# Reordering the first loads of a fused SSM and SwiGLU kernel

## The chip, the cores and the metric

The kernel runs on one core of one Trainium2 chip. The metric is the device time of one execution in microseconds (us); less is better. Three runs of the kernel before gave 200.62, 200.81 and 201.20 us, a median of 200.81 us.

## What is computed

A block of 2048 tokens with 512 features is normalized, and the normalized rows go through two branches whose results are added to the input:

```python
xn = layernorm(x)                                   # x: 2048 x 512, bf16
Lam_bar = exp(dt * Lam)                             # branch A: a diagonal complex state space model
Bu = xn @ B_bar.T                                   # 512 states
h[t] = Lam_bar * h[t-1] + Bu[t]                     # scan over the 2048 tokens
y = 2 * real(h @ C.T) + xn * Dskip
gate, up = xn @ w1, xn @ w3                         # branch B: 512 -> 1792, twice
glu = (silu(gate) * up) @ w2                        # 1792 -> 512
out = x + y + glu
```

All of it depends on the layer normalization, and the first thing that TensorE can do with data needs a piece of x, its statistics, and a piece of w1.

## The kernel before

The tokens are cut into four blocks of 512 (`TBLK`), each of four chunks of 128 tokens (`CPB`); the 1792 columns of w1 and w3 are cut into 14 tiles of 128 (`NFT`). For each block the GLU (`glu`, L587) multiplies the transposed, normalized block `xnT` by each tile of w1 and of w3 (four matmuls of 512 columns each), ScalarE takes the two sums out of PSUM (L596 with Silu, L597), VectorE multiplies them (L604). Between tiles stand the matmuls of the state space branch (`bu`), and behind block pairs the output products (`y_fast`). The order on each engine is written by hand in program order (`manual_schedule`); background work of VectorE is put between by a planner (`Filler`) with fixed costs. No order depends on when a transfer lands.

Block 0 is special, since nothing is there yet when it starts. Its first three tiles (`FIRST = 3`) are computed in quarters, chunk by chunk, as the data comes (`quarter`, L619). The order on the engines is this:

- VectorE: statistics of chunk 0 (L219, L220), of chunk 1, then the normalization (`ln_apply`, L224) of chunk 0 in two halves and of chunk 1, then statistics of chunks 2 and 3, then the normalization of chunks 2 and 3.
- ScalarE: its own DMA issues, a table load (L199), then Ln and Exp for 1/sqrt(variance) of each chunk (L233, L234), copies of the transposed chunks from PSUM to `xnT` (L244). After the first Exp comes an activation (L173) that writes one element of w1's later columns; the next weight load on SyncE's queue must wait for it, and so does all that SyncE issues behind it (`bulk_loads`).
- TensorE: ten matmuls on constants (`keep_busy`, L196), the transposes of chunk 0 (L243), four small ones on constants, the transposes of chunk 1, then L619 for chunk 0 on tiles 0 and 1 (eight matmuls with w1, eight with w3), for chunk 1 on the same tiles (16), the transpose of the state space parameters (L315), the transposes of chunk 2, chunk 0 on tile 2 (four with w1, four with w3), the transposes of chunk 3, chunk 1 on tile 2, and then chunks 2 and 3 on all three tiles. From tile 3 on the full width is used (L587).
- GpSimd: constants, three small loads of the state space parameters, and the parameters' arithmetic.

Loads are issued by two engines, SyncE (SP) and ScalarE (ACT); each issue takes its engine's queue some 0.4 to 0.5 us, and the data comes behind it on the 16 DMA engines. `load_w(f0, f1)` loads the columns f0 to f1 of w1 (L156) and of w3 (L157), by default both on SyncE's queue; with `0, 2 * P` that is tiles 0 and 1, with `2 * P, 4 * P` tiles 2 and 3, each piece 256 KB in runs of 512 bytes. A chunk of x is 128 KB in rows of 1 KB; chunks 0 and 1 are loaded in column halves. The first loads before are, in each queue's order:

| queue | loads |
|---|---|
| SyncE | chunk 0 left half, chunk 1 left half (L166), chunk 2 (L168), w1 then w3 of tiles 0 and 1, w1 then w3 of tiles 2 and 3 |
| ScalarE | chunk 0 right half, chunk 1 right half (L166), chunk 3 (L167) |

Behind these come, on SyncE's queue, w1 and w3 of tiles 4 to 7, block 1 of x (L162), the state space matrices by transposing DMA (L176, L177), the rest of w1 and w3, and so on. The loads share eight semaphores in turn, so each load from the ninth on waits, before it is issued, for the landing of the one eight places before it.

Of the kernel before, what the change touches and what calls it, by code (L numbers as in the profile page):

```python
# [17 lines left out]
P = 128  # L18
# [45 lines left out]
def kernel(  # L64
# [17 lines left out]
    nc = tc.nc  # L82
    _, S, D = A_x.shape
# [21 lines left out]
    D1, D2 = slice(0, DH), slice(DH, D)  # L105
# [3 lines left out]
    xv = A_x[0].rearrange("(c p) d -> p c d", p=P)  # L109
# [41 lines left out]
    x_blk = [x_all[:, i] for i in range(NBLK)]  # L151
# [3 lines left out]
    def load_w(f0, f1, eng1=nc.sync, eng3=nc.sync):  # L155
        eng1.dma_start(out=w1_sb[:, :, f0:f1], in_=w1v[:, :, f0:f1])  # L156
        eng3.dma_start(out=w3_sb[:, :, f0:f1], in_=w3v[:, :, f0:f1])  # L157
# [3 lines left out]
        for i in range(0, CPB, n):  # L161
            nc.sync.dma_start(out=x_blk[b][:, i:i + n, :], in_=xv[:, b * CPB + i:b * CPB + i + n, :])  # L162

    for c in range(2):
        for eng, dsl in ((nc.sync, slice(0, D // 2)), (nc.scalar, slice(D // 2, D))):
            eng.dma_start(out=x_blk[0][:, c, dsl], in_=xv[:, c, dsl])  # L166
    nc.scalar.dma_start(out=x_blk[0][:, 3, :], in_=xv[:, 3, :])  # L167
    nc.sync.dma_start(out=x_blk[0][:, 2, :], in_=xv[:, 2, :])  # L168
    load_w(0, 2 * P)
    load_w(2 * P, 4 * P)  # L170

    def bulk_loads():
# [1110 lines left out]
```

## Time and profile before

| what | value |
|---|---|
| median of three runs | 200.81 us (200.62 to 201.20) |
| profiled execution: span from the first to the last instruction | 199.5 us |
| median of the runs less that span | 1.3 us |
| granted clock of TensorE | 0.999 |
| busy share of the span: TensorE / VectorE / ScalarE / GpSimd | 98% / 91% / 68% / 26% |
| data moved by DMA | 25.12 MB, mean 126 GB/s |
| first matmul on data (L243) / first L619 / first L587 | 5.08 / 6.27 / 12.88 us |

The profile is of one execution; its page names its span and not a time of the whole execution, so the 1.3 us around the span are taken from the runs. PE in the views is TensorE, PEld its weight load, DVE is VectorE, ACT ScalarE, POOL GpSimd, SP SyncE; a q behind an engine's name is its queue. A timeline line gives the start, the time to the end, the engine, the line of the kernel, the operation, what it writes and reads, how many were merged, and in brackets how long the engine was idle before and what ended it. "DMA to landing" counts from the start of the issue to the last of the data.

### The profile page before, as it was taken

To read this page: it belongs to the slowest core of one execution; us is meant where nothing else is said; L and a number is where in the kernel's file an instruction comes from. 1 tells how busy PE (TensorE), PEld (TensorE's weight loads), DVE (VectorE), ACT (ScalarE), POOL (GpSimd) and SP (SyncE) were. 2 spreads that over 40 slices of the span, in tenths; PEclk is the share of its full clock that TensorE was granted. 3 is DMA by queue.
4 is the path that set the end of the run, shared out by engine and by line. 5 is a ranking of instruction groups with operands and counts; after the bars stand their busy time and mean duration, and the time that the engine had idled before them with its cause. 6 is when DMAs were issued, how large, how long until landed. Compare 5 with 4: busy or idle time off the path is not lost.

```text
span 199.5 us, 3700 instructions
## 1 busy us (share of the span) xinstructions
PE 195.6 (98%) x1401; PEld 130.7 (65%) x1401; DVE 181.8 (91%) x254; ACT 135.0 (68%) x281; POOL 51.5 (26%) x75
## 2 busy tenths in 40 slices
PE   8999999999999999999999999999999999999994
PEld 2774444444444488866555468888566678888893
DVE  3689699999999999989999997999999999999972
ACT  4699897699999996968998684362588783111220
POOL 7180289700411134041202305040021303310000
PEclk9999999999999999999999999999999999999999
DMA  4999996991497054730997455838137732941111
GB/s 138 326 277 200 302 186 124 343 273 23 69 181 141 0 105 82 135 105 0 156 148 119 89 92 98 172 83 132 53 59 129 149 56 52 174 92 36 53 44 40
DMA packets 32258, 25.12 MB, mean 126 GB/s; under 512 B 16240, under 2 KB 29936, under 8 KB 32240
## 3 DMA queue, kind: packets, MB, share of 16 engines
q0 software_dynamic: 6128, 11.38, 33.5%
q1 hardware_dynamic: 25536, 13.21, 26.8%
q10 hardware_dynamic: 576, 0.30, 0.5%
q8 instruction: 11, 0.18, 0.4%
q14 instruction: 7, 0.06, 0.1%
HBM read 7.74 MB, written 2.10 MB: 49 GB/s over the span
## 4 chain that ended last, share of the span: by engine, by line
PE 95%; DMA 2%; SPq 1%; issue 0%; DVE 0%
PE gu_ps L587 34%; PE gu_ps L1054 17%; PE y_ps L1054 10%; PE gu_ps L848 7%; PE bu_ps L1054 7%; PE bu_ps L454 3%; PE y_ps L454 3%; PE y_ps L869 3%; PE y_ps L780 3%; DMA w_sb<-in_B_w_dram 2%; PE gu_ps L619 2%; PE gu_ps L780 2%; PE bu_ps L869 1%; PE bu_ps L780 1%; PE bu_ps L619 1%; SPq L166 0%
## 5 line engine op out<-in xcount | busy, mean ns | idle before, releaser
L587 PE MATMUL gu_ps<-xnT,w_sb 128*128 128x512 bf16 x312 | 69.6, 379 | 0.0
L587 PEld LDWEIGHTS <-w_sb 128*128 128x128 bf16 x312 | 30.5, 98 | 34.2
L1054 PEld LDWEIGHTS <-act 128*128 128x128 f16 x462 | 43.5, 98 | 5.4
L596 ACT ACTIVATE g<-gu_ps 128x512 bf16<-128x512 f32 x41 | 24.8, 606 | 6.0 <-PE gu_ps L587 3.6
L597 ACT ACTIVATE u<-gu_ps 128x512 bf16<-128x512 f32 x41 | 24.8, 606 | 4.5 <-PE gu_ps L587 3.7
L505 DVE TENSOR_TENSOR_SCAN u<-rho,ends,u 128x512 bf16<-128x512 f32 x16 | 20.0, 1270 | 0.0
L527 POOL DMA_DIRECT2D act<-p x7 | 9.2, 1320 | 34.0 <-DVE act L519 22.1
L1054 PE MATMUL gu_ps<-w_sb,act 128*128 128x256 bf16 (+3 forms) x126 | 16.0, 267 | 0.0
L848 PE MATMUL gu_ps<-xnT,w_sb 128*128 128x512 bf16 x64 | 15.9, 379 | 0.0
L604 DVE TENSOR_TENSOR act<-g,u 128x1024 f16<-128x1024 bf16 x21 | 14.2, 679 | 0.4 <-ACT u L597 0.4
L860 ACT ACTIVATE g<-gu_ps 128x512 bf16<-128x512 f32 x14 | 8.4, 599 | 5.4 <-PE gu_ps L848 5.0
L454 PEld LDWEIGHTS <-bt 128*128 128x128 bf16 x64 | 6.3, 98 | 7.5
L1077 ACT ACTIVATE x_blk<-gu_ps 128x256 f32<-128x256 f32 (+1 forms) x9 | 3.3, 368 | 10.6 <-PE gu_ps L1054 10.6
L1054 PE MATMUL bu_ps<-w_sb,act 128*128 128x256 bf16 (+3 forms) x84 | 10.4, 264 | 0.0
L1054 PE MATMUL gu_ps<-ct,act 128*128 128x256 f16 (+1 forms) x72 | 10.4, 267 | 0.0
L848 PEld LDWEIGHTS <-w_sb 128*128 128x128 bf16 x64 | 6.3, 98 | 4.8
L505 DVE TENSOR_TENSOR_SCAN u<-rho,u 128x512 bf16<-128x512 f32 x8 | 9.2, 1206 | 0.0
L1054 PEld LDWEIGHTS <-x_blk 128*128 128x128 f16 x88 | 8.6, 98 | 1.0
L1054 PEld LDWEIGHTS <-tw 128*128 128x128 f16 x88 | 8.6, 98 | 1.0
L513 DVE TENSOR_TENSOR p<-u,tabe 128x2048 f16<-128x2048 bf16 (+1 forms) x8 | 8.7, 1085 | 0.1
L519 DVE TENSOR_TENSOR act<-u,tabe 128x2048 f16<-128x2048 bf16 (+1 forms) x8 | 8.7, 1083 | 0.0
L488 DVE TENSOR_TENSOR u<-u,tabe 128x2048 bf16<-128x2048 bf16 x7 | 8.5, 1219 | 0.1
(203 smaller groups left out, 392.5 us busy)
## 6 DMA issues: line engine op xcount, KB each, us to landing
act<-p POOLq DMA_DIRECT2D x6, 512.0 KB, 6.1
xn<-x_blk POOLq DMA_DIRECT2D x4, 512.0 KB, 5.5
out_dram<-xn SPq DMA_DIRECT2D x15, 128.0 KB, 1.7
w_sb<-in_B_w_dram SPq DMA_DIRECT2D x1, 1792.0 KB, 8.2
act<-act POOLq DMA_DIRECT2D x5, 352.0 KB, 4.6
w_sb<-in_B_w_dram SPq DMA_DIRECT2D x2, 768.0 KB, 6.4
u<-p POOLq DMA_DIRECT2D x3, 512.0 KB, 5.1
w_sb<-in_B_w_dram SPq DMA_DIRECT2D x4, 256.0 KB, 4.9
```

The source lines that it names most:

```text
L454: nc.tensor.matmul(out=ps, lhsT=bt[:, ri, dt, pt * P:(pt + 1) * P], rhs=xnT_blk[b][:, dt, :], start=(dt == 0), stop=(dt == NDT - 1))
L505: nc.vector.tensor_tensor_scan(out=v, data0=rho[:, pt:pt + 1].to_broadcast([P, TBLK]), data1=v, initial=init, op0=ALU.mult, op1=ALU.add)
L513: nc.vector.tensor_tensor(out=by_state(st["p16"][:, csl]), in0=by_chunk(st["g"][:, :, ::-1, tsl]), in1=by_chunk(tabe[:, psl, 2:0:-1, tsl]) ...
L519: nc.vector.tensor_tensor(out=by_state(act_state(b, hf)[:, csl]), in0=by_chunk(st["g"][:, :, :, tsl]), in1=by_chunk(tabe[:, psl, 0:1, tsl] ...
L527: gp.dma_start(out=a, in_=p16, accum_op=ALU.add)
L587: nc.tensor.matmul(out=ps[:, tsl], lhsT=w[:, dt, f * P:(f + 1) * P], rhs=xnT[:, dt, tsl], start=(dt == 0), stop=(dt == NDT - 1))
L596: nc.scalar.activation(out=g16[:, f % 2, :], in_=g_ps, func=ACT.Silu)
L597: nc.scalar.activation(out=u16[:, f % 2, :], in_=u_ps, func=ACT.Copy)
L604: nc.vector.tensor_tensor(out=act_gates(b, f - 1), in0=split(g16), in1=split(u16), op=ALU.mult)
L780: nc.tensor.matmul(out=out[:, h * TH:(h + 1) * TH], lhsT=left[:, h, k, :], rhs=right[:, k, :], start=(start and h == 0 and k == 0), stop=( ...
L848: nc.tensor.matmul(out=ps, lhsT=w[:, dt, f * P:(f + 1) * P], rhs=xnT[:, dt, :], start=(dt == 0), stop=(dt == NDT - 1))
L1054: nc.tensor.matmul(out=out, lhsT=left[:, k, :], rhs=right[k][:, cols], start=(start and k == 0), stop=(k == NK - 1), skip_group_check=True)
```

## The change

The first loads get another order and partly another queue. The sizes and the total are unchanged, but chunk 1 comes as one load instead of two halves, so there is one load less. Nothing else is changed: the order of the instructions on TensorE, VectorE and GpSimd and of the computing ones on ScalarE is that of before.

```diff
-    for c in range(2):
-        for eng, dsl in ((nc.sync, slice(0, D // 2)), (nc.scalar, slice(D // 2, D))):
-            eng.dma_start(out=x_blk[0][:, c, dsl], in_=xv[:, c, dsl])
-    nc.scalar.dma_start(out=x_blk[0][:, 3, :], in_=xv[:, 3, :])
-    nc.sync.dma_start(out=x_blk[0][:, 2, :], in_=xv[:, 2, :])
-    load_w(0, 2 * P)
+    def load_chunk(c, eng, dsl=slice(0, D)):
+        eng.dma_start(out=x_blk[0][:, c, dsl], in_=xv[:, c, dsl])
+
+    load_chunk(0, nc.sync, D1)
+    load_chunk(0, nc.scalar, D2)
+    load_chunk(1, nc.scalar)
+    load_w(0, 2 * P, nc.sync, nc.scalar)
+    load_chunk(2, nc.sync)
+    load_chunk(3, nc.sync)
     load_w(2 * P, 4 * P)
```

The queues' new order:

| queue | loads |
|---|---|
| SyncE | chunk 0 left half, w1 of tiles 0 and 1, chunk 2, chunk 3, w1 then w3 of tiles 2 and 3 |
| ScalarE | chunk 0 right half, chunk 1, w3 of tiles 0 and 1 |

Line numbers behind the change are higher by three in the changed kernel (L619 becomes L622, and so on).

## The prediction

> **What bounds the kernel now.** I read first the waits of TensorE over the whole execution, because the chain that ended last is 95% PE:
>
> ```profile
> PE 95%; DMA 2%; SPq 1%; issue 0%; DVE 0%
> ...
> PE bu_ps L196 <- PEq L1267: 0.8, 1, 0.8
> PE gu_ps L619 <- DMA w_sb<-in_B_w_dram: 0.3, 1, 0.3
> PE y_ps L243 <- DVE xn L224: 0.2, 1, 0.2
> ...
> PEld L619 <- DMA w_sb<-in_B_w_dram: 0.6, 2, 0.4
> ```
>
> These are all of its waits but for weight loads behind the warm-up and before the first transposes. None lies after 10 us: from there to 197 us TensorE is never listed as waiting, so a stall removed at the head should reach the end in full, and one added there as well. Only the first 10 us matter. Next, the timeline of TensorE there, on which L619 is the GLU of block 0 on its first three tiles:
>
> ```profile
> 5.86 0.40 PE L243 MATMUL y_ps<-ident,xn 128*128 128x128 bf16 x4
> 6.27 0.62 PE L619 MATMUL gu_ps<-xnT,w_sb 128*128 128x128 bf16 x8
> 7.16 1.51 PE L619 MATMUL gu_ps<-xnT,w_sb 128*128 128x128 bf16 x24 [0.27 <-DMA w_sb<-in_B_w_dram]
> 8.61 0.18 PE L315 MATMUL y_ps<-ident,par_rows 12*128 12x12 bf16 x1
> 8.71 0.40 PE L243 MATMUL y_ps<-ident,xn 128*128 128x128 bf16 x4
> 8.95 0.74 PE L619 MATMUL bu_ps<-xnT,w_sb 128*128 128x128 bf16 x8
> ```
>
> Eight such matmuls take 0.45 us elsewhere (24 in 7.16 to 8.61 are 0.06 each). So there are three weight stalls: 0.18 before 6.27 (transposes through at 6.09), 0.44 before 7.16, and a hidden one in the last line, where the same eight matmuls are 0.74 long instead of 0.61: 0.13. They answer to landings. Issue start plus time to landing gives w1 of tiles 0, 1: 2.11+4.1 = 6.2; w3: 2.58+4.5 = 7.1; w1 of tiles 2, 3: 3.13+5.2 = 8.3; w3: 3.69+5.6 = 9.3. The rows, L156 (w1), L157 (w3), then L168 (chunk 2, issued 1.64) and L167 (chunk 3, 1.65):
>
> ```profile
> DMA to landing us min/median/max: 4.1/5.2/5.9
> ...
> DMA to landing us min/median/max: 4.5/5.6/6.9
> ...
> DMA to landing us min/median/max: 3.7/3.7/3.7
> ...
> DMA to landing us min/median/max: 4.0/4.0/4.0
> ```
>
> The sum to win is 0.18+0.44+0.13 = **0.75 us**, but the third stall is the catch: whatever comes before it, TensorE can't pass 9.3 until the second w3 piece has landed. Last, what the DMA engines did (the last two columns are their busy share and GB/s):
>
> ```profile
> 2.00:3.00 1.00, 1.00 (x4) 0.44 (x3) 0.00 (x0) 0.87 (x1) 1.00 (x3) 1.00 1.15 272
> 3.00:4.00 1.00, 1.00 (x4) 0.29 (x2) 0.89 (x3) 0.41 (x1) 0.93 (x3) 1.00 0.47 154
> 4.00:5.00 1.00, 0.92 (x3) 0.15 (x1) 0.96 (x4) 0.85 (x4) 0.61 (x3) 1.00 0.82 250
> 5.00:6.00 1.00, 0.91 (x11) 0.60 (x12) 0.89 (x4) 0.92 (x4) 0.00 (x0) 1.00 1.13 329
> ```
>
> From 5 us on they are full (about 0.31 MB per us); between 3 and 5 they idled (1-0.47)+(1-0.82) = 0.71 us. The second w3 piece ends a queue of 1.5 MB (x 512 KB, four weight pieces of 256 KB); the change alters the order within it, not its size.
>
> **The change part by part.** *Issues.* SyncE issues six loads up to the second w3 piece instead of seven (about 0.45 us each), so the first w1 piece goes out at 1.17 instead of 2.11, the second pair at about 2.6 and 3.1 instead of 3.13 and 3.69. ScalarE still issues three; the third now is a weight piece, which took 0.51 on SyncE against 0.45 for chunk 3. Its table load starts at 2.2 instead of 2.13 and ends by 3.5; the first Ln waits until 4.09 (0.68 idle), which hides it. There is one DMA less, so each later load waits for another of the first ones (the ninth from the start on waits for the one eight before it). The second w3 piece waits for half of chunk 0 (lands by 3), block 1's x for w1's first piece: 6.2 at the latest, against an issue at 6.05, and its data is read at 18. SyncE waits for ScalarE's activation of 4.65 to 4.85 either way, so everything from 4.88 on keeps its time. No compute instruction is added or moved.
>
> *First weights.* w1 by its old time to landing: 1.17+4.1 = 5.3, below the 6.09 at which TensorE wants it. w3 by its own: 1.65+4.5 = 6.15, below 6.54. Even if neither ran faster than before, the first two stalls go: TensorE reaches the parameter transpose at 7.99 instead of 8.61 (its rows land at 2.78+4.5 = 7.3, in time).
>
> *What is late next.* It would then want the second w3 piece at 9.17-0.62 = 8.55; the old time is 9.3. If the DMA engines idle as long as before, that landing stays and the whole 0.62 is handed back as one wait: gain 0. If they don't idle at all, it comes 0.71 earlier, 8.6: gain 0.7, with the bound of 0.75. For the idle's end: a weight piece stands on each queue by 2 us, while before chunks 2 and 3 stood there with weights behind them. Against it: chunks of 1 KB rows are among what moves then in both orders, and nothing shows what the idle came from. I take half, **0.35 us**, bounds 0 and 0.7.
>
> [...]
>
> *Chunk 1 whole on ScalarE's queue.* Its halves landed 2.1 to 2.4 after issue, by 3.5; VectorE takes it at 3.90, after chunk 0. Bounds for the whole: 2.1 (it lands at 3.3) and that of w3, 4.5 (5.7). Nearest are chunk 0's halves, which have its place in the queue, and chunk 3, which has its shape (4.0, so 5.1). I take 4.3, a little below the middle. Behind it on VectorE stand both applies of chunk 0, and behind those the transposes and all of L619; so from 3.9 on each us of its lateness moves TensorE by one. But the 0.75 of removed stalls absorb it: until 4.65 nothing is lost against before, and 4.3 asks for the second w3 at 8.95, about where I put it (9.3-0.35).
>
> *Chunks 2 and 3 behind w1.* They landed at 5.4 and 5.6; VectorE wants them at 5.72 and 6.54. Now they follow w1 on SyncE's queue: 5.3 plus the 256 KB of both, 0.8 at 0.31 MB per us, beside w3 on the other queue: 5.7 to 6.5. From the start of chunk 3's statistics (6.54) to the third tile's w3 the old times give 0.80 to the apply of chunk 2 (7.34), 0.41 for it, 0.22 for its transposes and 0.24 for four matmuls: 1.7; from the start of chunk 2's statistics 0.8 more. So they cost nothing against 9.3 until chunk 3 lands at about 7.55, or chunk 2 at 6.7.
>
> **Sum.** 199.5 us of span less 0.35 is 199.15. The page gives no time of the profiled execution outside its span; the runs' median of 200.81 lies 1.3 above it (1.1 to 1.7 by the three). With 1.3: **200.5 us**.
>
> **The rivals.**
> - *The forecast, partial recovery:* one wait at the second w3 piece stays; gain 0 to 0.6, 200.2 to 200.8. It takes in "the change does nothing", where the stalls merely move to 9.3. Chance 0.43.
> - *Full recovery:* the DMA idle goes, no weight wait over 0.1 us is left: gain 0.6 to 0.75, 200.1. For it: w1 and w3 are early by every row, and only 0.71 us of idle has to go. Against: all 1.5 MB must move without a gap. Chance 0.32.
> - *Slower, by chunk 1:* its 1 KB rows share the engines with w1's 512 packets and land as chunk 3 did or later. At 5.1 TensorE is 5.1+0.05-3.90 = 1.25 late against 0.75 removed: +0.5, 201.3; at 5.7, +1.1, 201.9. It decides from 4.65 on; I price it 201.5. The trace has 2.4 for halves with this place against it. Chance 0.17.
> - *Slower, by chunks 2 and 3* held behind w1: at 7.5 for chunk 2 (w1's longest time, 5.9, from 1.64) +0.8, 201.6. Chance 0.08.
>
> **How the numbers follow.** About 0.3% (0.6 us) is what a measurement can tell from no change here. Faster: the second case, 0.32. Slower: both last ones, 0.25. Same: the first, 0.43, which alone runs from 200.2 to 200.8. The range goes from 199.9 (0.75 gained, 1.1 around the span, rounded) to 201.6, leaving out the later half of the slow cases and a rest below.
>
> **What would show it.** Right: TensorE's wait list has no wait for weights before 8 us, and one near 8.9 for the bu_ps matmuls of L619's third tile; the second w3 piece lands at 8.6 to 9.2; the DMA share from 3 to 5 us rises above 0.47 and 0.82. Full recovery: that wait is gone as well. Slower: VectorE waits for x before its second statistics, over 0.75 us, or before the third, over 1 us. Wrong altogether: a wait of TensorE after 10 us that takes the gain back, or the head moved by 0.5 with an end that isn't.

## The result and the profile after

The changed kernel is slightly slower: a median of 201.71 us (201.35 to 203.65, 14 runs) against 200.95 us for the kernel before (200.62 to 201.67, 14 runs). The ratio of the means is 1.0053, with an interval of 1.0036 to 1.0069. Four of the 14 runs of after are apart from the rest, at 202.77 to 203.65; the other ten average 201.65. The profiled execution of after has a span of 199.8 us and took 201.67, so 1.87 us lie around the span, where the prediction had 1.3.

First the waits of TensorE in the profile of after, over the whole execution (columns: us in total, times, longest us), with the wait for x that stands above them:

```profile
DVE stats L222 <- DMA x_blk<-in_A_x_dram: 3.9, 2, 3.1
...
PEld L246 <- DVE xn L227: 2.0, 2, 1.8
...
PE y_ps L246 <- DVE xn L227: 0.9, 1, 0.9
...
PE bu_ps L199 <- PEq L1270: 0.8, 1, 0.8
```

Every wait for weights is gone. In their place TensorE waits for normalized rows: its weight load for the first transposes is idle 1.8 us (0.80 in the profile of before). VectorE's wait for x has a second part besides chunk 0's 3.1. The timeline of before has, at the same places:

```profile
3.90 0.67 DVE L219 BATCH_NORM_STATS2 stats<-x_blk 128x6 f32<-128x512 bf16 x1
...
5.08 0.54 PE L243 MATMUL y_ps<-ident,xn 128*128 128x128 bf16 x4 [0.16 <-DVE xn L224]
```

and the timeline of after:

```profile
4.86 0.69 DVE L222 BATCH_NORM_STATS2 stats<-x_blk 128x6 f32<-128x512 bf16 x1 [0.86 <-DMA x_blk<-in_A_x_dram]
...
6.06 0.54 PE L246 MATMUL y_ps<-ident,xn 128*128 128x128 bf16 x4 [0.87 <-DVE xn L227]
...
7.07 1.95 PE L622 MATMUL gu_ps<-xnT,w_sb 128*128 128x128 bf16 x32
...
9.30 0.61 PE L622 MATMUL bu_ps<-xnT,w_sb 128*128 128x128 bf16 x8
...
13.10 1.24 PE L590 MATMUL gu_ps<-xnT,w_sb 128*128 128x512 bf16 x4
```

The second statistics start at 4.86 instead of 3.90: chunk 1 landed at 4.84, 3.7 us after its issue. TensorE's first transposes begin at 6.06 instead of 5.08, and the GLU at 7.07 instead of 6.27. From there the 32 matmuls run through without a stall, and the eight on the second w3 piece take 0.61 and not 0.74. The full width (L590) begins at 13.10 instead of 12.88. The chain that ended last, in order of time in after's first microseconds (start, us, what), says the same; it goes from that one transfer through VectorE into TensorE:

```profile
1.15 3.69 DMA x_blk<-in_A_x_dram
4.84 0.02 issue
4.86 0.70 DVE stats L222
...
7.24 1.79 PE gu_ps L622 x32
```

The first weights did come earlier. The landings of w1 (L156) and w3 (L157) in after:

```profile
DMA to landing us min/median/max: 3.8/5.1/5.7
...
DMA to landing us min/median/max: 4.6/5.8/7.2
```

With the issues at 1.19 and 1.65 that is 5.0 for the first w1 and 6.3 for the first w3, against 6.2 and 7.1 in before. The second pieces landed at 7.85 and 8.48, where this profile of before had 8.38 and 9.25; a second profile of before (before_again, below) has 7.54 and 8.39, so for these pieces the change is not shown to have won anything. The stretches of after (last two columns: busy share of the DMA engines and GB/s):

```profile
2.00:3.00 1.00, 1.00 (x4) 0.44 (x3) 0.00 (x0) 0.78 (x1) 1.00 (x3) 1.00 0.52 145
3.00:4.00 1.00, 1.00 (x4) 0.29 (x2) 0.88 (x2) 0.50 (x1) 0.93 (x3) 1.00 0.99 286
4.00:5.00 1.00, 1.00 (x3) 0.15 (x1) 0.14 (x2) 0.70 (x3) 0.62 (x3) 1.00 1.12 349
```

The idle share between 3 and 5 us is gone (0.47 and 0.82 became 0.99 and 1.12), but part of it moved ahead: from 2 to 3 us the share fell from 1.15 to 0.52. That is where chunk 1 would have had to come; its first packet started at 3.09, almost two microseconds after its issue at 1.15.

### The profile page after: what moved, and what is told of

The parts are those of the page before. It is cut to its first block, busy times and chain, and to the rows that moved or that the text cites. A ratio compares the mean times of both kernels' runs of the same rounds, so it can differ in the third digit from the quotient of the medians.

```text
span 199.8 us, 3685 instructions
## 1 busy us (share of the span) xinstructions
PE 194.7 (97%) x1388; PEld 130.7 (65%) x1401; DVE 181.8 (91%) x254; ACT 135.1 (68%) x281; POOL 51.8 (26%) x75
## 2 busy tenths in 40 slices
DMA packets 32114, 25.12 MB, mean 126 GB/s; under 512 B 16224, under 2 KB 29792, under 8 KB 32096
## 4 chain that ended last, share of the span: by engine, by line
PE 95%; DMA 2%; DVE 1%; issue 0%; ACTq 0%
PE gu_ps L590 33%; PE gu_ps L1057 17%; PE y_ps L1057 10%; PE gu_ps L851 7%; PE bu_ps L1057 7%; PE bu_ps L457 3%; PE y_ps L457 3%; PE y_ps L872 3%; PE y_ps L783 3%; DMA x_blk<-in_A_x_dram 2%; PE gu_ps L622 2%; PE gu_ps L783 2%; PE bu_ps L872 1%; PE bu_ps L783 1%; PE bu_ps L622 1%; PE y_ps L246 1%
## 5 line engine op out<-in xcount | busy, mean ns | idle before, releaser
L590 PE MATMUL gu_ps<-xnT,w_sb 128*128 128x512 bf16 x304 | 68.9, 379 | 0.4
L590 PEld LDWEIGHTS <-w_sb 128*128 128x128 bf16 x312 | 30.5, 98 | 34.2
L851 PE MATMUL gu_ps<-xnT,w_sb 128*128 128x512 bf16 x61 | 15.6, 379 | 0.1
L222 DVE BATCH_NORM_STATS2 stats<-x_blk 128x6 f32<-128x512 bf16 x8 | 5.4, 678 | 3.9 <-DMA x_blk<-in_A_x_dram 3.9
```

The lines of the kernel that those rows point to most:

```text
L590: nc.tensor.matmul(out=ps[:, tsl], lhsT=w[:, dt, f * P:(f + 1) * P], rhs=xnT[:, dt, tsl], start=(dt == 0), stop=(dt == NDT - 1))
L851: nc.tensor.matmul(out=ps, lhsT=w[:, dt, f * P:(f + 1) * P], rhs=xnT[:, dt, :], start=(dt == 0), stop=(dt == NDT - 1))
```

## The experiments

Three theories stood at the start. **A**: chunk 1 is late because w1's first piece, 512 packets of 512 bytes (256 KB), now moves beside it from the other queue (the expectation of e1 supposes how: its descriptors are made behind those 512; no view shows where they are made). **B**: a whole chunk of 1 KB rows on one queue is late in any company. **C**: the loss lies behind the head, and the moved start is not what costs.

The kernels differ from after or before only in the first loads or in the number of warm-up matmuls (NWARM, 10 in after). One table for all profiles; "2nd" and "3rd" are the starts of VectorE's second statistics and its idle time for x before the third, "GLU" TensorE's first GLU matmul, "full" its first of full width:

| kernel | beside chunk 1 on the other queue | 2nd | 3rd idle | GLU | full | span |
|---|---|---|---|---|---|---|
| before | its own other half | 3.90 | 0 | 6.27 | 12.88 | 199.5 |
| before_again | its own other half | 3.76 | 0 | 6.25 | 12.28 | 198.9 |
| after | w1, 256 KB | 4.86 | 0 | 7.07 | 13.10 | 199.8 |
| after_again | w1, 256 KB | 4.21 | 0.20 | 6.42 | 12.46 | 199.2 |
| e1 | its own other half | 3.89 | 0.92 | 6.34 | 12.85 | 199.5 |
| e2 | chunk 2, 128 KB | 4.15 | 0 | 6.44 | 12.46 | 199.2 |
| e10 (e2 again) | chunk 2, 128 KB | 4.16 | 0 | 6.38 | 12.40 | 199.1 |
| e6 | its own other half | 4.06 | 0 | 6.34 | 12.37 | 199.0 |
| e3 | w1, 256 KB | 5.49 | 0 | 7.99 | 14.85 | 201.5 |
| e7 | w1, 256 KB | 5.68 | 0 | 7.89 | 13.92 | 200.6 |
| e8 | w1, 256 KB | 4.70 | 0 | 6.91 | 12.93 | 199.7 |
| e4 | other columns of w1, 320 KB | 5.39 | 0 | 7.61 | 13.63 | 200.3 |
| e5 | narrow columns of w1, 64 KB | 4.82 | 0 | 7.04 | 13.06 | 200.1 |
| e9 | w1's first quarter, 64 KB | 4.12 | 0.81 | 6.62 | 12.98 | 200.0 |

The last two columns answer C for the profiled executions: span less "full" is 186.6 to 186.8 in twelve profiles (187.0 in e5 and e9). Whatever the head loses or wins by 13 us is there at the end, and nothing behind gives it back.

**e1: chunk 1 in halves on both queues again.** Against after:

```diff
-    load_chunk(1, nc.scalar)
+    load_chunk(1, nc.sync, D1)
+    load_chunk(1, nc.scalar, D2)
```

> Chunk 1 again as two column halves, one on each queue, ahead of the weights; all else as in the changed kernel. Theory A (chunk 1 is late because its descriptors are made behind the 512 of w1's piece, issued at the same time on the other queue): chunk 1 lands by 3.6 us, VectorE's second statistics start at 3.9 instead of 4.86, the first GLU matmul starts at 6.1 to 6.3 instead of 7.07, the time falls by 0.8 to 1.0 us from the changed kernel, to 200.7 to 200.9 (the kernel before: 200.95). Theory B (a whole chunk in 1 KB rows on one queue is late whatever stands beside it): the same here, since the chunk is halved. Theory C (the loss is not in the head but behind it, by the changed waits of SyncE's later loads): the head recovers and the time stays at 201.5 or more.

Measured: 201.38 (11 runs) against 201.11 for before (23 runs), ratio 1.0011 (1.0002 to 1.0020). Chunk 1 came in time (3.54), but the time is 0.5 us above the 200.9 expected at most; the timeline of e1 shows who was late next:

```profile
6.71 0.69 DVE L223 BATCH_NORM_STATS2 stats<-x_blk 128x6 f32<-128x512 bf16 x1 [0.92 <-DMA x_blk<-in_A_x_dram]
...
8.77 0.40 PE L247 MATMUL y_ps<-ident,xn 128*128 128x128 bf16 x4 [0.36 <-DVE xn L228]
```

The first line is the third statistics: chunk 2, still behind w1, landed at 6.69, and the transposes of chunk 2 wait for it. So most of the loss goes with chunk 1 (the median is 0.27 us above before's, against 0.76 for after), and the prediction's other slow rival, chunk 2 behind w1, is the next bound.

**e2: chunk 1 whole on ScalarE's queue as in after, but w1 behind chunk 2.**

```diff
-    load_w(0, 2 * P, nc.sync, nc.scalar)
     load_chunk(2, nc.sync)
+    load_w(0, 2 * P, nc.sync, nc.scalar)
     load_chunk(3, nc.sync)
```

> Chunk 1 stays whole on ScalarE's queue; on SyncE's queue w1's first piece changes places with chunk 2, so that next to chunk 1 a load of 128 descriptors is issued and not one of 512. Theory A: chunk 1 lands at 3.5 to 4.0 us, the second statistics start by 4.0, time 200.7 to 201.0. Theory B: chunk 1 still lands at 4.6 or later, time 201.4 or more. Theory C: 201.5 or more with a good head.

Measured: 200.92 (12 runs) against 201.11, ratio 0.9988 (0.9977 to 0.9998). In the timeline of e2 chunk 1 is hardly late (it landed at 4.13; 4.0 at most was expected):

```profile
4.15 0.69 DVE L222 BATCH_NORM_STATS2 stats<-x_blk 128x6 f32<-128x512 bf16 x1 [0.26 <-DMA x_blk<-in_A_x_dram]
...
6.44 1.95 PE L622 MATMUL gu_ps<-xnT,w_sb 128*128 128x128 bf16 x32
```

The same whole load on the same queue, with another neighbour, is in time. That speaks for A and against B. One profile alone would not carry this, since chunk 1 landed at 4.84 and at 4.18 in two profiles of after itself (after_again, below). The spans of all runs do: 19 of the 24 runs of this order (e2 and e10) have a span of 199.4 us or less, and 2 of the 26 runs of after.

**e3: the other half of that test.** Chunk 1 in two column halves, both on ScalarE's queue, w1 second on SyncE's.

```diff
-    load_chunk(1, nc.scalar)
+    load_chunk(1, nc.scalar, D1)
+    load_chunk(1, nc.scalar, D2)
```

> Chunk 1 as two column halves, both on ScalarE's queue, w1's first piece second on SyncE's as in the changed kernel. Theory A: the packet size does not matter, both halves come behind w1's descriptors; the last lands at 4.6 or later, time 201.4 to 202.0. Theory B: halves of 512 bytes land by 3.9 (the second is issued 0.4 later), time 201.0 or less.

Measured: 203.39 (6 runs) against 201.11, ratio 1.0111 (1.0088 to 1.0135). In the timeline of e3:

```profile
5.49 0.69 DVE L223 BATCH_NORM_STATS2 stats<-x_blk 128x6 f32<-128x512 bf16 x1 [1.48 <-DMA x_blk<-in_A_x_dram]
...
6.70 0.65 PE L247 MATMUL y_ps<-ident,xn 128*128 128x128 bf16 x4 [1.51 <-DVE xn L228]
...
7.99 2.79 PE L623 MATMUL gu_ps<-xnT,w_sb 128*128 128x128 bf16 x32
```

Rows of 512 bytes did not help, so the row size is not the cause: A again. But the loss is larger than the landing explains. The 32 matmuls took 2.79 us instead of 1.95: TensorE still ran at the slow rate of its warm-up (weight loads of up to 147 ns there, 147 in the warm-up, 98 at most in after). e7 takes that up.

**before_again: the kernel before once more, with a profile.**

> The kernel before once more, for a second profile. Its profiled execution had a span of 199.5 us, and the changed kernel's runs lie 1.8 above their spans; if the same holds for the kernel before, the median of 200.95 belongs to a span of about 199.1, and the profile that the prediction was made from had 0.4 us more of weight stalls than a usual run. Expected if so: a span of 199.0 to 199.2 and weight stalls of 0.2 to 0.4 us instead of 0.75. Otherwise: 199.5 again, with 0.7 of stalls.

Measured: 200.79, span 198.9. Its timeline:

```profile
6.25 1.96 PE L619 MATMUL gu_ps<-xnT,w_sb 128*128 128x128 bf16 x32
...
8.48 0.61 PE L619 MATMUL bu_ps<-xnT,w_sb 128*128 128x128 bf16 x8
...
12.28 1.46 PE L587 MATMUL gu_ps<-xnT,w_sb 128*128 128x512 bf16 x5
```

None of the three weight stalls is there, not even in part. In this execution w1 landed at 5.83 and 7.54, w3 at 6.65 and 8.39; in the profile that the prediction read, 6.22 and 8.38, 7.11 and 9.25. The stalls belonged to one execution. Over 80 further runs of before the span goes from 198.9 to 200.0 with a median of 199.3, and 22 of them are at 199.5 or above: that profile was a somewhat slow one, and this is one of the fastest.

**e4 and e5: what in the neighbour counts, its packets or its bytes?** e4 puts a load of 128 long runs (2,560 bytes, 320 KB of other columns of w1) second on SyncE's queue; e5 cuts the first w1 and w3 pieces so that 512 short packets (128 bytes, 64 KB) stand beside chunk 1; the rest of w1's piece follows on that queue at 1.65. For e4:

```diff
+    nc.sync.dma_start(out=w1_sb[:, 1, 4 * P:F], in_=w1v[:, 1, 4 * P:F])
     load_chunk(1, nc.scalar)
```

and for e5:

```diff
+    nc.sync.dma_start(out=w1_sb[:, :, 0:P // 2], in_=w1v[:, :, 0:P // 2])
     load_chunk(1, nc.scalar)
-    load_w(0, 2 * P, nc.sync, nc.scalar)
+    load_w(P // 2, 2 * P, nc.sync, nc.scalar)
+    nc.scalar.dma_start(out=w3_sb[:, :, 0:P // 2], in_=w3v[:, :, 0:P // 2])
```

> The changed kernel with one more load put second on SyncE's queue, beside chunk 1: 128 rows of 2560 bytes of w1's later columns (320 KB in 128 descriptors; the same columns are loaded again later as before). So more bytes stand beside chunk 1 than in the changed kernel (256 KB), in a quarter of the descriptors. Only chunk 1's landing is of interest. If what delays it is the number of descriptors of the load beside it: it lands at 4.0 to 4.3 us, as beside chunk 2. If it is the bytes that share the DMA engines: at 4.9 or later (4.84 in the changed kernel). The total time is no measure, since 320 KB are added.

> The changed kernel with the first pieces of w1 and w3 each cut in two column parts, the narrow one (64 columns) of w1 second on SyncE's queue: 512 descriptors of 128 bytes, 64 KB, beside chunk 1; the other parts follow. By the number of descriptors: chunk 1 lands at 4.6 to 5.0 us, as in the changed kernel. By bytes: at 4.2 or earlier.

Measured: e4 202.06, e5 201.91, one run each. Chunk 1 landed at 5.37 in e4 and at 4.80 in e5. The timelines, e4 and then e5:

```profile
5.39 0.69 DVE L223 BATCH_NORM_STATS2 stats<-x_blk 128x6 f32<-128x512 bf16 x1 [1.59 <-DMA x_blk<-in_A_x_dram]
```

```profile
4.82 0.69 DVE L224 BATCH_NORM_STATS2 stats<-x_blk 128x6 f32<-128x512 bf16 x1 [0.86 <-DMA x_blk<-in_A_x_dram]
```

Neither explanation holds alone: by the number of packets e4 should have been early, by the bytes e5. The trace records a landing in 16 steps. The fifteenth of chunk 1 came at 3.87 in e5 (64 KB beside it), 3.96 in e2 (128 KB), 4.76 in after (256 KB) and 4.71 in e4 (320 KB), which looks like bytes; but after_again, with the same 256 KB beside it, has 3.85. The last step decides the landing, and it came 0.9 behind the fifteenth in e5, 0.7 in e4, 0.3 in after_again and 0.1 in after. So which property of the neighbour delays chunk 1, packets and bytes together perhaps, and what holds the last step back, is not settled here.

**e6: all of x first, chunk 1 in halves, w1 ahead of chunk 3 only.** Against after:

```diff
-    load_chunk(1, nc.scalar)
-    load_w(0, 2 * P, nc.sync, nc.scalar)
+    load_chunk(1, nc.sync, D1)
+    load_chunk(1, nc.scalar, D2)
     load_chunk(2, nc.sync)
+    load_w(0, 2 * P, nc.sync, nc.scalar)
     load_chunk(3, nc.sync)
```

> Chunk 1 in halves on both queues as in the kernel before, then chunk 2 on SyncE's queue ahead of w1's first piece, w3's first piece third on ScalarE's queue, chunk 3 behind w1. If only late x chunks cost the changed kernel its time, no wait for x is left here: chunk 1 by 3.6, chunk 2 by 5.7, chunk 3 by 6.5, and no wait for weights over 0.1 us; time as the kernel before or up to 0.3 us less. If the pieces of w beside x delay it in any order, chunk 2 lands after 6 us and the time is 0.2 to 0.5 us above the kernel before.

Measured: 200.93 (12 runs) against 201.17 (17 runs), ratio 0.9990 (0.9978 to 1.0002). The timeline of e6:

```profile
4.06 0.69 DVE L223 BATCH_NORM_STATS2 stats<-x_blk 128x6 f32<-128x512 bf16 x1 [0.16 <-DMA x_blk<-in_A_x_dram]
```

Chunk 1 landed at 4.04, later than the 3.6 expected, and VectorE waits 0.16 us for it; TensorE has no wait for weights. Yet nothing measurable is won: with its head in order the kernel is where before's good executions are.

**e7: e3 with 14 warm-up matmuls instead of 10**, so that TensorE is not idle while it waits for chunk 1.

```diff
-    NWARM = 10
+    NWARM = 14
```

> The kernel with chunk 1 as two halves on ScalarE's queue (its time 1.1% above the kernel before), with 14 instead of 10 matmuls on constants at the start, which fill TensorE's wait of 1.5 us. There 32 matmuls of the GLU took 2.79 us and a weight load 147 ns instead of 98. If the slow rate comes from TensorE having stood idle: 1.95 us and 98 ns here, and a time of 0.9 to 1.3 us less, 202.1 to 202.5, though chunk 1 lands as late as before. If it comes from late weights or from ScalarE: no change.

Measured: 202.51 (4 runs) against 201.17, ratio 1.0055 (1.0036 to 1.0075); e3 had 203.39. The timeline of e7:

```profile
5.68 0.69 DVE L223 BATCH_NORM_STATS2 stats<-x_blk 128x6 f32<-128x512 bf16 x1 [1.76 <-DMA x_blk<-in_A_x_dram]
...
7.89 1.95 PE L623 MATMUL gu_ps<-xnT,w_sb 128*128 128x128 bf16 x32
```

Chunk 1 is later than in e3, and the GLU's 32 matmuls take 1.95 again instead of 2.79. So e3's extra loss was TensorE's slow rate, and it went when the idle time ahead of chunk 0's transposes was cut (at TensorE's weight load 2.41 us in e3, 0.89 in e7). Idle time alone is not enough for it: in e4 TensorE waited 1.41 us there, against 1.51 in e3, and was at its full rate. The two kernels ran on different chips, each beside its own runs of before, which differ by 0.06.

**after_again: the changed kernel once more.**

> The changed kernel once more, unchanged, for a second profile and for its spread beside the next kernel on the same chip. Its earlier runs had ten spans of 199.6 to 200.2 us and four of 201.0 to 201.9. Expected again: a median ratio of about 1.004 to the kernel before, chunk 1 landing at 4.5 to 5.0, and some runs over 202.5.

Measured: 201.64 (12 runs, 201.04 to 202.99) against 201.06 (23 runs), ratio 1.0033 (1.0016 to 1.0050). The profile fell on its fastest run, 201.04. The timeline:

```profile
4.21 0.69 DVE L222 BATCH_NORM_STATS2 stats<-x_blk 128x6 f32<-128x512 bf16 x1 [0.21 <-DMA x_blk<-in_A_x_dram]
...
6.42 1.95 PE L622 MATMUL gu_ps<-xnT,w_sb 128*128 128x128 bf16 x32
```

Here chunk 1 landed at 4.18, outside what was expected, and the span is 199.2: the same kernel with chunk 1 0.66 earlier is 0.6 shorter. That is not the usual run: the median span of the twelve is 199.85, that of the first profile, which by the same step puts chunk 1 near 4.85.

**e8: after with two more warm-up matmuls (NWARM 12).**

> The changed kernel with 12 instead of 10 matmuls on constants, which end about 0.9 us later and fill TensorE's wait for chunk 1. If the changed kernel's high runs are those in which TensorE stood idle long enough to fall to its slow rate: no run above 202.3, the median within 0.15 of the changed kernel's. If the high runs have another cause, a quarter of them stays above 202.5.

Measured: 201.56 (12 runs, 201.29 to 202.01) against 201.06, ratio 1.0024 (1.0013 to 1.0035). No run is above 202.01, where the two sets of after have 5 of 26 at 202.77 and more. That fits a tail made by the slow rate, but at 5 in 26 twelve runs would be free of it by chance 8 times in 100, and no profile caught such a run.

**e9: w1's first piece as four loads of 64 KB**, one for each group of 128 rows, so that less of it stands beside chunk 1.

```diff
-    load_w(0, 2 * P, nc.sync, nc.scalar)
+    for t in range(NDT):
+        nc.sync.dma_start(out=w1_sb[:, t, 0:2 * P], in_=w1v[:, t, 0:2 * P])
+    nc.scalar.dma_start(out=w3_sb[:, :, 0:2 * P], in_=w3v[:, :, 0:2 * P])
```

> The changed kernel with w1's first piece issued as four loads of 128 descriptors (64 KB each, 0.4 to 0.5 us apart) instead of one of 512, the same bytes; chunks 2 and 3 are issued 1.3 us later for it. If what stands beside chunk 1 in the DMA engines while it moves delays it, there is less of it: chunk 1 lands at 3.9 to 4.3 instead of 4.84. If the whole of w1's piece has to pass first in any case: 4.7 or later. The time is not the measure, since chunks 2 and 3 come later.

Measured: 201.78, one run. The timeline of e9:

```profile
4.12 0.69 DVE L224 BATCH_NORM_STATS2 stats<-x_blk 128x6 f32<-128x512 bf16 x1
...
6.85 0.70 DVE L224 BATCH_NORM_STATS2 stats<-x_blk 128x6 f32<-128x512 bf16 x1 [0.81 <-DMA x_blk<-in_A_x_dram]
```

Chunk 1 is as early as beside chunk 2, with the whole of w1 in the queue but in smaller loads. Chunk 2, now issued behind four loads at 3.06, pays instead, as in e1.

**e10: e2 once more**, to see whether it beats both kernels.

> The kernel with w1's first piece behind chunk 2 once more, to see whether its small lead over the kernel before (ratio 0.9988, interval 0.9977 to 0.9998) holds in other runs. If it is real: a ratio of 0.998 to 0.9995 again, with chunk 1 landing by 4.2. If it was the draw: 1.000 within 0.001.

Measured: 201.07 (12 runs) against 201.10 (17 runs), ratio 1.0008 (0.9988 to 1.0029). e2's small lead does not come again. One of its runs took 203.33, as high as the high runs of after, though the profiled run of this kernel has chunk 1 at 4.14. No order tried here is shown to be faster than before.

## Why the prediction was wrong, step by step

It said 200.5 us, range 199.9 to 201.6, with 0.32 for faster, 0.43 for no change and 0.25 for slower. The medians came out slower by 0.76 us, and 201.71 lies 0.1 above the range. What happened is the rival "slower, by chunk 1", which had a chance of 0.17 and a price of 201.5. That the price came so near is in part luck: it was made for a landing at 5.1 or later, where the profile has 4.84, and with 1.3 us around the span, where 1.87 were.

- **Only the first 10 us matter: right.** Span and start of the full width move together in all profiles.
- **First weights early: right.** 5.0 and 6.3 us against 5.3 and 6.15 predicted; the first two stalls went, but before_again has none either.
- **Second w3 by half of the idle, 8.6 to 9.2: earlier than that, but not shown to be won by the change.** It landed at 8.48, 0.77 before the 9.25 of the profile read, and no wait for weights was left. But before_again has it at 8.39 without the change, with DMA shares of 0.76 and 1.01 from 3 to 5 us instead of 0.47 and 0.82. The late pieces and most of the idle belonged to the execution that was read. No run shows a gain here. The bytes stayed the same (25.12 MB in both profiles); what changed was which of them moved in the early microseconds, and x paid for it (chunk 1 at 4.84 instead of 3.52).
- **Chunk 1 at 4.3: the step that failed.** It was chosen between 3.3 and 5.7 "a little below the middle", near chunk 0's halves, which have the place in the queue, rather than chunk 3 with the shape. Neither takes in what stands beside the load, which the rival with 0.17 did, and in which the late orders differ from the others. With w1's whole first piece second on SyncE's queue, chunk 1 was complete at 4.18 to 5.59 in five profiles (after, after_again, e8, e3, e7); with x there, or a quarter of w1, at 3.50 to 4.14 in seven. From its issue that is 3.7 us beside w1 in after (4.84), 3.0 and 3.5 in the other two profiles of this order; 3.0 beside chunk 2; and 2.1 to 2.4 in halves on both queues in before. In the table a later second statistics moves the full width one for one: "full" less "2nd" is 8.23 to 8.31 in all nine profiles in which chunk 1 landed after 4.0, chunk 2 was at most 0.2 late and TensorE at its full rate by the GLU (8.24 in after; e9 and e3 are the two that this leaves out). The missed 0.54 us is the larger part of the span's error: 199.8 against 199.15, or 0.65.
- **Break-even at 4.65: right for the profile, wrong for the kernel.** With 8.25 from the second statistics to the full width, the read profile's 12.88 gives 4.63. The median span of before, 199.3, means a full width near 12.65 and a break-even of 4.4; before_again's 12.28 gives 4.0. "The sum to win is 0.75" was measured on an execution with more stall than most.
- **1.3 us around the span: wrong.** In the 80 runs it is 1.72 to 1.93, and 1.87 in after. The prediction set the span of one execution against the median of others; the 0.57 between 1.3 and 1.87 is the rest of its error, and was a sign that the profiled execution was slower than the median run: of the three runs at hand only the slowest, 201.20, lies 1.7 above 199.5. With 1.87, its own span of 199.15 would have been 201.0, no change against 200.95.
- **Chunks 2 and 3 behind w1 cost nothing until 6.7: right for after** (chunk 2 at 5.34 and 6.30), because chunk 1 was late too. With chunk 1 repaired it is the bound: e1 has chunk 2 at 6.69 and its median is 0.27 us above before's.
- **Not thought of: the slow rate.** In e3 a wait of 1.51 us ahead of the first transposes went with a slow start to 9.74 us, against 4.15 to 6.70 in the other profiles (e4, with a wait of 1.41, among them). After's ten lower runs average 0.60 above before's mean of 201.05; the four high ones raise that to 1.07, the ratio's 0.53%. That these four are the slow rate is an inference from e3, e7 and e8, not seen in a profile. In size it fits in part: e3's profile lost 1.12 us to it (9.36 from second statistics to full width against 8.24), and the spans of the four, 201.0 to 201.9, are 1.2 to 2.1 above the 199.8 of the profile of after.

## What to carry to other kernels

Stalls of a few tenths at the head, read from one profile, may belong to that execution: compare its time less its span with several runs, and take a second profile before counting a stall as something to win. Moving a load ahead on one queue was paid for here by what the other queue moved at that moment (the first w1 at 5.0 instead of 6.22, chunk 1 at 4.84 instead of 3.52); before moving weights forward, ask which load the first compute chain hangs on, and try it with large loads kept from beside it. In e3, where TensorE was not yet at its full rate, a late chunk 1 cost 1.12 us more than its lateness (9.36 from second statistics to full width, 8.24 in after).

## What the runs showed of the hardware

**TensorE starts slow, and when it speeds up is not the program's alone.** In its first microseconds a weight load takes 0.15 us (147 ns, L200 of e3) and a transpose 0.11; later 0.10 (98 ns, L623) and 0.06 (four at L247 in 0.65 and then in 0.40). The trace's record of the granted clock begins with the first full rate, at 4.15 to 6.70 us into the span in thirteen of the fourteen profiles and at 9.74 in e3; one and the same kernel, before, has it at 4.51 and at 6.22. The granted-clock column of the stretches does not show the slow part (it reads 1.00 in after from 2 us on); the weight loads do. e3 and then e4, both after a like wait, the weight loads of the four small matmuls between the transposes:

```profile
7.03 0.47 PEld L200 LDWEIGHTS <-const-bfloat16-1.0 128*128 128x128 bf16 x4
```

```profile
6.92 0.27 PEld L200 LDWEIGHTS <-const-bfloat16-1.0 128*128 128x128 bf16 x4
```

TensorE's weight load had been idle for 2.41 us in e3 and for 2.31 in e4; e4 was at its full rate and e3 not until 9.74. The step of the transposes is by about two, and it comes at differing times. By the record of the clock the full rate then lasts 194.56 us in before and in after, which have it from 4.51 and from 5.58. What decides when the rate rises is not shown: waits of nearly one length ahead of the first transposes, 1.51 us of idle TensorE in e3 and 1.41 in e4, went with a rise at 9.74 and with the full rate by 6.92.

**The head differs from execution to execution.** In before the first weights and chunks 2 and 3 landed 0.4 to 0.9 us apart in two profiles of one kernel (chunk 3 at 5.60 and 4.69, second w3 at 9.25 and 8.39), and chunk 1 in after at 4.84 and 4.18. From one profile of each, landings of first loads that differ by less than about 0.9 us say nothing of an order of loads; the spans of many runs do.

**A pause of the DMA engines moved with the order.** A stretch in which they are little used is at 3 to 4 us in before (0.47) and at 2 to 3 us in after (0.52). Over all profiles the share from 2 to 3 us is 0.52 to 0.66 in the five with w1's whole first piece second on SyncE's queue and 0.73 to 1.15 in the other nine. The transfers from 2.5 to 3.0 us in before, and then in after (packets, MB; for the queue q10 packets, MB and share):

```profile
DMA packets 261, 0.13 MB, mean 259 GB/s; under 512 B 34, under 2 KB 261, under 8 KB 261
...
q10 hardware_dynamic: 149, 0.07, 46.3%
```

```profile
DMA packets 77, 0.04 MB, mean 71 GB/s; under 512 B 8, under 2 KB 77, under 8 KB 77
...
q10 hardware_dynamic: 10, 0.00, 2.2%
```

The queue named q10 is ScalarE's: over the span it moved 0.30 MB in before and 0.49 MB in after, as much as that engine issues (288 and 480 KB). With w1 on SyncE's queue it moved ten packets in that time instead of 149 (65 in after_again). The start is not fixed by the order: chunk 1, issued at 1.15 in both, moved its first packet at 3.09 in after and at 2.38 in after_again. Why it starts so late, and at such different times, is left open.
